# Gated linear attention and MLP in one kernel: the first four blocks loaded as two pairs with two tokens a partition, the squared activations laid out by block

## The chip, the core and the metric

The kernel runs on one core of one Trainium2 chip. The metric is the device time of one execution in microseconds, the median of several runs. The engines are named as in the profile: PE (matmul), PEld (its weight loads), DVE (vector), ACT (scalar, activation functions), POOL (GpSimd), SP (issues most DMAs). PSUM is the memory that PE writes, in banks of 512 fp32 columns.

## The reference

Four batches of eight heads, 768 tokens, 48 values a head. A recurrent state is decayed row by row with alpha and updated by k and v; its product with q goes, heads side by side, into an MLP with a squared ReLU.

```python
batch, n_heads, seq, head_dim = (4, 8, 768, 48)
n_tokens, d_model, d_ff = (3072, 384, 2048)
for t in range(S):
    state = alpha[:, :, t, :, None] * state + np.einsum('bhd,bhe->bhde', k[:, :, t], v[:, :, t])
    y[:, :, t] = np.einsum('bhd,bhde->bhe', q[:, :, t], state)
x = y.transpose(0, 2, 1, 3).reshape(B * S, H * D)
h = x @ w_in
r = np.maximum(h, 0.0)
g = s * (r * r) + b
out = g @ w_out
```

## The kernel before

The 3,072 tokens are cut into 24 **blocks** of 128 tokens, six to a batch. A token of a block lies on each partition. For every block:

- SP loads alpha, q, k, v with one DMA each into `a_in` to `v_in` (L192, five buffers each, `NIN`). One DMA moves 192 KB in 1,024 pieces of 192 bytes, a head's 48 fp32 values of one token.
- ACT takes the logarithm (L299), PE sums it over the tokens with a triangular matrix and makes the block's total decay `bl` with small matmuls (L304), both in PSUM bank `ct_ps`. ACT makes b = exp(sum), 1/b and exp(total) (L319, L322).
- DVE multiplies q by b and k by 1/b into `qk` (L332, L337). Both are transposed into `qkT`: blocks 0 to 7 (`NPE`) on PE through `ct_ps` with a copy by DVE (L345, L372), later ones by a DMA that ACT issues (L354).
- POOL casts v into `vp` (L326). PE multiplies k and v for the state update into bank `py_ps` (KV, L360); DVE adds it to the state (t1, L380), POOL applies the decay (L396).
- PE makes the scores in `a_ps` (A, L402), DVE masks them (L414), PE multiplies by v and adds the state's part, again in `py_ps` (y, L433). ACT evicts y to `xd` (L466), the MLP's input. From block 9 on (`NAY`), y of a block is issued just behind A of the next one.

The MLP runs over **groups** of one or two blocks (`GROUPS`, L18), whose `xd` has three buffers. A *unit* of mm1 (L484) is one PSUM bank of 512 columns, four feature tiles of 128 for a group of one block (matmuls of 128 columns) or two for a group of two (256 columns). ACT applies the ReLU (L498), DVE squares (L501), one instruction for each feature tile, into `gt`: sixteen tiles, one for each feature tile, each a ring of 12 blocks. mm2 (L509) takes four feature tiles at a time (a quarter) and accumulates 384 columns in one of two `o_ps` banks; DVE scales and adds the bias (L522), SP stores (L534).

Weights come through four staging buffers `wst` of 768 KB, are cast by ACT (L247, L260), and for w_out DVE also sums them over the rows for the bias (L267 to L273), which two fp32 matmuls then finish (L285).

The order is written by a small planner (`Schedule`, L43): every operation has an engine, an assumed duration, a priority and the names it reads and writes; the planner runs this list in its own time and issues the instructions in the order found. The priorities are `want(n)`, from the block's number, `UNIT` and `LEAD`, plus an offset for each kind of operation in `P`. SP's loads have their order from `LOADS` and then from the block's number; stores have a high priority and stand in SP's queue where the planner saw their data ready. Each engine executes its queue in order. Where PE would be idle early on, the planner adds filler matmuls on zeros into `o_ps[0]` (L684).

Of the kernel before, what the change touches and what calls it, by code (L numbers as in the profile page):

```python
# [15 lines left out]
VW = 144  # L16

GROUPS = [2, 1, 1, 2, 2, 2, 2, 2, 2, 2, 2, 2, 2]  # L18
UNIT = 0.756
LEAD = {1: 98.3, 2: 224.9, 4: 115.8}  # L20

NPE = 8

NAY = 9
# [5 lines left out]
TB = 1.02  # L30
TW = 2.15
FILL_GAP = 0.45

P_BM, P_CS, P_BMM = -5, -380.7, 485.1
P = dict(
    ln=-4.98, cum=7.29, eb=-25.15, ei=-13.19, vc=29.56, qb=-11.01, kb=-39.87, T=15.87,
    Tc=-9.38, KV=-36.89, t1=-9.91, sn=53.95, Ay=-1.22, A=-16.47, mk=-35.05, y=52.89,
    ye=4.82, m1=-13.73, re=-0.8, sq=-9.48, m2=-14.41, oe=20.18,
)

LOADS = ["k1", "q1", "a1", "i0", "k2", "v1", "i1", "a2", "i2", "q2", "i3", "v2", "a3", "q3", "k3", "o0", "v3", "a4", "o1", "o2", "k4", "o3", "q4", "z0", "v4"]
# [92 lines left out]
def kernel(  # L134
# [16 lines left out]
    C = 128  # L151
    NCH = S // C
# [17 lines left out]
    p_ps = py_ps[:, 0:384].rearrange("a (p e) -> a p e", p=NP)  # L170
    y_ps = py_ps[:, 0:384].rearrange("a (k t) -> a k t", k=3)
    h_ps = [ps.tile([128, 512], FP32, name=f"h_ps{i}") for i in range(2)]
    o_ps = [ps.tile([128, 512], FP32, name=f"o_ps{i}") for i in range(2)]

# [9 lines left out]

    a_in = many("a_in", NIN, [128, H, D], FP32)
# [4 lines left out]
    b_col = sb.tile([128, 1], FP32, name="b_col")  # L190

# [7 lines left out]
    for src, dst in ((alpha, a_in), (q, q_in), (k, k_in), (v, v_in)):  # L199
        load(0, src, dst)  # L200
    nc.scalar.preload_act_table_set("natural_log_exp_and_others")

    la_sb = many("la", 2, [128, H, 64], BF16, zero=nc.vector)
    U_bf = sb.tile([128, 128], BF16, name="U_bf")
    make_upper_triangular(nc, U_bf, 1.0, diag=True)
    ident_bf = sb.tile([128, 128], BF16, name="ident_bf")
    make_identity(nc, ident_bf)
    zeros = sb.tile([128, 512], BF16, name="zeros")
    nc.vector.memset(zeros, 0.0)
    ones_col_bf = sb.tile([128, 1], BF16, name="ones_col_bf")  # L210
    nc.vector.memset(ones_col_bf, 1.0)
    vp_sb = many("vp", 4, [128, NP, VW], BF16, zero=nc.gpsimd)
    mask = sb.tile([128, 128], BF16, name="mask")
    make_upper_triangular(nc, mask, 1.0, diag=True)
    b_sb = many("b_s", 2, [128, H, D], FP32)
    binv_sb = many("binv", 2, [128, H, D], FP32)
    qk_sb = many("qk", 3, [128, 2, H, 64], BF16, zero=nc.vector)
    qkT_sb = many("qkT", 3, [128, 2, NP, 128], BF16)
    am_sb = many("am", 2, [128, 2, NP, 128], BF16)
    blast_sb = many("blast", 2, [128, NP], BF16)  # L220
    t1_sb = many("t1", 2, [128, NP, 96], BF16, zero=nc.gpsimd)
    s_sb = many("s_st", 3, [128, NP, 96], BF16, zero=nc.gpsimd)
    xd_sb = many("xd", 3, [128, 3, 512], BF16)
    r_sb = many("r", 2, [128, 512], BF16)
    gt_sb = [sb.tile([128, RING * C], BF16, name=f"gt{j}") for j in range(NJ)]
# [49 lines left out]

    def load_bs():
        nc.sync.dma_start(out=b_col, in_=moe_b.to_broadcast((128, 1)))
        nc.sync.dma_start(out=s_col, in_=moe_s.to_broadcast((128, 1)))
# [6 lines left out]
    def bias_mm():  # L285
        for e in range(2):
            nc.tensor.matmul(
                out=o_ps[1][:, 0:d_model],
                lhsT=bones,
                rhs=colsum[:, d_model * e : d_model * (e + 1)],  # L290
                start=(e == 0),
                stop=(e == 1),
            )

    def bias_copy():
        nc.vector.tensor_copy(out=bias_w, in_=o_ps[1][:, 0:d_model])
# [7 lines left out]
    def st_cum(n):  # L304
        la = la_sb[n % 2]
        nc.tensor.matmul(  # L306
            out=cum_ps, lhsT=U_bf, rhs=la[:, :, 0:D], start=True, stop=True
        )
        laf = la.rearrange("a h d -> a (h d)")
        for p in range(NP):  # L310
            nc.tensor.matmul(  # L311
                out=bl_ps[:, p : p + 1],
                lhsT=laf[:, 128 * p : 128 * p + 128],
                rhs=ones_col_bf,
                start=True,
                stop=True,
            )
# [4 lines left out]
    def st_exp_i(n):  # L322
        nc.scalar.activation(out=binv_sb[n % 2], in_=cum_ps, func=AF.Exp, scale=-1.0)  # L323
        nc.scalar.activation(out=blast_sb[n % 2], in_=bl_ps, func=AF.Exp)
# [7 lines left out]
    def st_qb(n):  # L332
        nc.vector.tensor_tensor(  # L333
            out=qk_sb[n % 3][:, 0, :, 0:D], in0=q_in[n % NIN], in1=b_sb[n % 2], op=ALU.mult
        )

    def st_kb(n):  # L337
        nc.vector.tensor_tensor(  # L338
            out=qk_sb[n % 3][:, 1, :, 0:D],
# [5 lines left out]
    def st_T(n):  # L345
        f = qk_sb[n % 3].rearrange("a x h d -> a (x h d)")
# [7 lines left out]
    def st_Tdma(n):  # L354
        nc.scalar.dma_start_transpose(  # L355
            out=qkT_sb[n % 3].rearrange("a x p t -> a (x p) t"),
            in_=qk_sb[n % 3].rearrange("a x h d -> a (x h d)"),
        )

    def st_KV(n):  # L360
        kb = qk_sb[n % 3][:, 1].rearrange("a h d -> a (h d)")
        vp = vp_sb[n % 4].rearrange("a p (x d) -> a p x d", d=D)
        for p in range(NP):
            nc.tensor.matmul(  # L364
                out=p_ps[:, p, :],
# [6 lines left out]
    def st_Tcopy(n):  # L372
        nc.vector.tensor_copy(  # L373
            out=qkT_sb[n % 3].rearrange("a x p t -> a (x p t)"),
# [5 lines left out]
    def st_t1(n):  # L380
        bl = blast_sb[n % 2].unsqueeze(2).to_broadcast([128, NP, D])
        for e in range(2):
            r, c = slice(64 * e, 64 * e + 64), slice(D * e, D * e + D)
            if n % NCH == 0:
                nc.vector.tensor_tensor(
                    out=s_sb[n % 3][r, :, c], in0=p_ps[r, :, c], in1=bl[r], op=ALU.mult
                )
            else:
                nc.vector.tensor_tensor(  # L389
                    out=t1_sb[n % 2][r, :, c],  # L390
                    in0=p_ps[r, :, c],
# [10 lines left out]
    def st_A(n):  # L402
        qkT = qkT_sb[n % 3]
# [10 lines left out]
    def st_mask(n):  # L414
# [3 lines left out]
            in1=mask.unsqueeze(1).to_broadcast([128, H, 128]),  # L418
# [14 lines left out]
    def st_y(n):  # L433
        first = n % NCH == 0
        qT = qkT_sb[n % 3][:, 0]
# [6 lines left out]
        for i, (p, e, x) in enumerate(parts):  # L442
            c0 = 32 * x - 96 * p
            nc.tensor.matmul(  # L444
                out=y_ps[32 * (x % 4) : 32 * (x % 4) + 32, x // 4, :],
# [15 lines left out]

    blk_group = []
# [3 lines left out]
    def st_yevac(n):  # L466
        g, t = blk_group[n]
        nc.scalar.activation(  # L468
            out=xd_sb[g % 3][:, :, t * C : (t + 1) * C], in_=y_ps, func=AF.Copy
        )  # L470
# [30 lines left out]
    def square(w):  # L501
        g, js = units[w]
        n = GROUPS[g] * C
        c0 = first_blk[g] % RING * C
        for i, j in enumerate(js):
            r = r_sb[w % 2][:, i * n : (i + 1) * n]
            nc.vector.tensor_tensor(out=gt_sb[j][:, c0 : c0 + n], in0=r, in1=r, op=ALU.mult)  # L507

    def mm2(x):  # L509
        g, tt, jq = quads[x]  # L510
        op = o_ps[(x // 4) % 2]
        c0 = (first_blk[g] + tt) % RING * C
        for j in range(4 * jq, 4 * jq + 4):
            nc.tensor.matmul(  # L514
                out=op[:, 0:d_model],
                lhsT=gt_sb[j][:, c0 : c0 + C],
# [40 lines left out]
    SRC = {"a": (alpha, a_in), "q": (q, q_in), "k": (k, k_in), "v": (v, v_in)}  # L557
    loads = list(LOADS)
    for n in range(1, NBLK):
# [4 lines left out]

    stage = 0
    for x in range(4):
        op("SP", 1.4 if x == 0 else 0.85, -2000 + x, lambda: None, w=[("aqkv"[x], 0)], lat=2.0)
    for rank, item in enumerate(loads):
        t, i = rank - 1000, int(item[1:])
        if item[0] in "aqkv":  # L570
            if i < NIN:
# [18 lines left out]
    op("PE", 1.3, P_BMM, bias_mm, r=["bones", "colsum"], w=[("o", 1)], lat=0.16)  # L590
    op("DVE", 0.53, -300, bias_copy, r=[("o", 1)], w=["bias"])

    ys = {}

    def yevac_op(n):
        g = blk_group[n][0]
        op("ACT", 0.41, want(n) + P["ye"], st_yevac, n, r=["py"], w=[("xd", g % 3, blk_group[n][1])])
# [3 lines left out]
    def add_block(n):  # L601
        i2, i3, ii = n % 2, n % 3, n % NIN
        t = want(n)
        if n >= NIN:
# [6 lines left out]
        op("POOL", 0.5, t + P["vc"], st_vcast, n, r=[("v", ii)], w=[("vp", n % 4)], lock=True)  # L611
        op("DVE", 0.48, t + P["qb"], st_qb, n, r=[("q", ii), ("b", i2)], w=[("qb", i3)], lock=True)
        op("DVE", 0.48, t + P["kb"], st_kb, n, r=[("k", ii), ("bi", i2)], w=[("kb", i3)], lock=True)
        if n < NPE:
            op("PE", 0.45, t + P["T"], st_T, n, r=[("qb", i3), ("kb", i3)], w=["ct"], lat=0.16)
            op("DVE", 0.61, t + P["Tc"], st_Tcopy, n, r=["ct"], w=[("qkT", i3)])
        else:
            op("ACT", 1.25, t + P["T"], st_Tdma, n, r=[("qb", i3), ("kb", i3)],
               w=[("tq", i3), ("qkT", i3)], lat=0.1)
# [101 lines left out]
```

## Time and profile before

| | us |
|---|---|
| median of 7 runs (range) | 194.19 (193.9 to 194.84) |
| the profiled execution | 194.22 |
| its span, from first to last instruction | 192.3 |
| mm1 matmuls (L490) busy, x624 | 75.0 |
| mm2 matmuls (L514) busy, x384 | 72.6 |
| squares (L507, DVE) busy, x208 | 54.1 |
| ReLU (L499, ACT) busy, x96 | 56.1 |
| first mm1 matmul starts | 18.98 |

The busy time of matmuls holds overlaps, since they are pipelined: the distance between the starts of two neighbours is what one costs. The DMA section of the page shows loads of 192 KB with 3.8 to 4.4 us from issue to landing, weight loads of 768 KB with 7.6 to 7.9, and 117,536 of 124,218 packets under 512 bytes. The mean granted PE clock is 0.991.

### The profile page before, as it was taken

Reading aid. Unit: us, or ns where it says so; the run is one execution under the profiler, and the core shown is the slowest. Engines: PE = TensorE matmul, PEld = TensorE weight load, DVE = VectorE, ACT = ScalarE, POOL = GpSimd, SP = SyncE. Lnnn points to the kernel's source line nnn. Section 1 sums busy time; section 2 is a strip of 40 time slices with the busy share of each in tenths; the row PEclk is TensorE's granted clock in tenths of the full one; section 3 lists DMA queues with packets and bytes.
Section 4 is the critical chain, followed back from the end, with each engine's and each line's share of the span. In section 5 each row is a group of like instructions: output and inputs, shape, how many; then the busy total and the mean of one; then the engine's idle time right before and its main releaser. Section 6 shows DMA issues by size and latency. Waiting matters only on the chain.

```text
span 192.3 us, 5473 instructions
## 1 busy us (share of the span) xinstructions
PE 175.5 (91%) x2153; PEld 126.5 (66%) x2153; DVE 145.5 (76%) x368; ACT 109.0 (57%) x225; POOL 33.6 (17%) x60
## 2 busy tenths in 40 slices
PE   1885988979999999999999989999999999999992
PEld 1454766656677767677776667776776776777660
DVE  4742489999999999878788769778789787745421
ACT  4255779975356837278457538573674563664300
POOL 8411021123111420200122112100311321000000
PEclk9999699999999999999999999999999999999999
DMA  6999899999799999899898999997989884101112
GB/s 127 236 273 316 236 248 279 342 175 195 160 239 180 211 202 196 181 207 224 164 232 93 193 193 230 180 204 132 242 170 206 164 180 99 41 3 43 41 47 80
DMA packets 124218, 34.44 MB, mean 179 GB/s; under 512 B 117536, under 2 KB 122656, under 8 KB 124192
## 3 DMA queue, kind: packets, MB, share of 16 engines
q1 hardware_dynamic: 107296, 29.89, 69.2%
q10 hardware_dynamic: 16896, 4.20, 14.5%
q8 instruction: 17, 0.28, 0.6%
q14 instruction: 9, 0.07, 0.1%
HBM read 25.17 MB, written 4.72 MB: 155 GB/s over the span
## 4 chain that ended last, share of the span: by engine, by line
PE 61%; DVE 16%; DMA 7%; SPq 6%; ACT 3%; issue 3%; ACTq 2%; DVEq 0%
PE o_ps L514 25%; PE h_ps L490 24%; DVE gt L507 6%; DMA wst<-in_moe_w_in_dram 4%; PE py_ps L444 4%; SPq L194 4%; DMA k_in<-in_k_dram 3%; PE a_ps L406 3%; SPq L240 2%; DVE am L415 2%; DVE t L389 2%; PE py_ps L364 2%; ACTq L355 2%; PE ct_ps L306 2%; ACT r L499 1%
## 5 line engine op out<-in xcount | busy, mean ns | idle before, releaser
L490 PE MATMUL h_ps<-xd,w_in_bf 128*128 128x256 bf16 (+1 forms) x624 | 75.0, 267 | 2.1 <-ACT r L499 2.0
L499 ACT ACTIVATE r<-h_ps 128x512 bf16<-128x512 f32 x96 | 56.1, 599 | 35.8 <-PE h_ps L490 19.3
L514 PE MATMUL o_ps<-w_out_bf,gt 128*128 128x384 bf16 x384 | 72.6, 326 | 1.2 <-ACT w_out_bf L261 1.2
L507 DVE TENSOR_TENSOR gt<-r 128x256 bf16<-128x256 bf16 (+1 forms) x208 | 54.1, 310 | 14.8 <-ACT r L499 14.3
L490 PEld LDWEIGHTS <-w_in_bf 128*128 128x128 bf16 x624 | 55.6, 98 | 13.1 <-issue 2.8
L514 PEld LDWEIGHTS <-gt 128*128 128x128 bf16 x384 | 35.9, 98 | 20.2 <-issue 1.5
L415 DVE TENSOR_TENSOR am<-a_ps,mask 128x1024 bf16<-128x1024 f32 x24 | 29.3, 1221 | 2.6 <-PE a_ps L406 2.3
L327 POOL CAST vp<-v_in 128x384 bf16<-128x384 f32 x24 | 14.1, 586 | 72.3 <-DMA v_in<-in_v_dram 57.6
L400 POOL TENSOR_TENSOR s_st<-t,blast 128x384 bf16<-128x384 bf16 x16 | 14.2, 887 | 53.0 <-DVE t L389 24.8
L300 ACT ACTIVATE la<-a_in 128x384 bf16<-128x384 f32 x24 | 12.5, 520 | 13.7 <-DMA a_in<-in_alpha_dram 8.3
L525 DVE SCALAR_TENSOR_TENSOR o_sb<-o_ps,s_col,bias_w 128x384 f32<-128x384 f32 x24 | 14.8, 615 | 6.3 <-PE o_ps L514 6.0
L338 DVE TENSOR_TENSOR qk<-k_in,binv 128x384 bf16<-128x384 f32 x24 | 13.4, 557 | 6.5 <-ACT binv L323 4.4
L333 DVE TENSOR_TENSOR qk<-q_in,b_s 128x384 bf16<-128x384 f32 x24 | 13.3, 553 | 5.8 <-ACT b_s L320 4.6
L468 ACT ACTIVATE xd<-py_ps 128x384 bf16<-128x384 f32 x24 | 11.8, 492 | 10.0 <-PE py_ps L444 7.6
L320 ACT ACTIVATE b_s<-ct_ps 128x384 f32<-128x384 f32 x24 | 11.8, 491 | 8.5 <-PE ct_ps L311 7.1
L389 DVE TENSOR_TENSOR t<-py_ps,s_st 64x192 bf16<-64x192 f32 x32 | 11.3, 352 | 4.4 <-PE py_ps L364 3.1
L306 PE MATMUL ct_ps<-la,U_bf 128*128 128x384 bf16 x24 | 8.1, 335 | 6.4 <-POOL mask masks.py:65 4.1
L323 ACT ACTIVATE binv<-ct_ps 128x384 f32<-128x384 f32 x24 | 11.8, 491 | 0.0
L311 PEld LDWEIGHTS <-la 128*128 128x128 bf16 x96 | 6.0, 98 | 7.4 <-issue 5.5
L406 PE MATMUL a_ps<-qkT 64*128 64x128 bf16 x192 | 9.7, 222 | 1.2 <-DVE qkT L373 1.2
L406 PEld LDWEIGHTS <-qkT 64*128 64x128 bf16 x192 | 5.5, 95 | 7.7 <-issue 5.1
L444 PE MATMUL py_ps<-am,vp 128*32 128x128 bf16 x384 | 9.6, 219 | 0.7 <-DVE am L415 0.7
(42 smaller groups left out, 106.6 us busy)
## 6 DMA issues: line engine op xcount, KB each, us to landing
a_in<-in_alpha_dram SPq DMA_DIRECT2D x24, 192.0 KB, 4.3
q_in<-in_q_dram SPq DMA_DIRECT2D x24, 192.0 KB, 4.2
k_in<-in_k_dram SPq DMA_DIRECT2D x24, 192.0 KB, 3.8
v_in<-in_v_dram SPq DMA_DIRECT2D x24, 192.0 KB, 4.4
out_dram<-o_sb SPq DMA_DIRECT2D x24, 192.0 KB, 2.1
wst<-in_moe_w_in_dram SPq DMA_DIRECT2D x4, 768.0 KB, 7.9
wst<-in_moe_w_out_dram SPq DMA_DIRECT2D x4, 768.0 KB, 7.6
qkT<-qk ACTq DMA_TRANSPOSE x16, 4.5
```

The costliest lines, as they stand in the source:

```text
L327: nc.gpsimd.tensor_copy(out=vp_sb[n % 4].rearrange("a p (x d) -> a p x d", d=D)[:, :, 0:3:2, :], in_=v_in[n % NIN].rearrange("a (p e) d -> ...
L338: nc.vector.tensor_tensor(out=qk_sb[n % 3][:, 1, :, 0:D], in0=k_in[n % NIN], in1=binv_sb[n % 2], op=ALU.mult,)
L389: nc.vector.tensor_tensor(out=t1_sb[n % 2][r, :, c], in0=p_ps[r, :, c], in1=s_sb[(n - 1) % 3][r, :, c], op=ALU.add,)
L400: nc.gpsimd.tensor_tensor(out=s_sb[n % 3], in0=t1_sb[n % 2], in1=bl, op=ALU.mult)
L406: nc.tensor.matmul(out=a_ps[:, e, p, :], lhsT=qkT[64 * e : 64 * e + 64, 1, p, :], rhs=qkT[64 * e : 64 * e + 64, 0, p, :], start=True, stop ...
L415: nc.vector.tensor_tensor(out=am_sb[n % 2].rearrange("a e p t -> a (e p) t"), in0=a_ps.rearrange("a e p t -> a (e p) t"), in1=mask.unsquee ...
L444: nc.tensor.matmul(out=y_ps[32 * (x % 4) : 32 * (x % 4) + 32, x // 4, :], lhsT=(st[:, p, c0 : c0 + 32] if e is None else vp[:, p, c0 + 48 ...
L490: nc.tensor.matmul(out=hp[:, i * n : (i + 1) * n], lhsT=w_in_bf[:, kk, 128 * j : 128 * (j + 1)], rhs=xd_sb[g % 3][:, kk, 0:n], start=(kk = ...
L499: nc.scalar.activation(out=r_sb[w % 2], in_=h_ps[w % 2], func=AF.Relu)
L507: nc.vector.tensor_tensor(out=gt_sb[j][:, c0 : c0 + n], in0=r, in1=r, op=ALU.mult)
L514: nc.tensor.matmul(out=op[:, 0:d_model], lhsT=gt_sb[j][:, c0 : c0 + C], rhs=w_out_bf[:, j, :], start=(j == 0), stop=(j == NJ - 1),)
L525: nc.vector.scalar_tensor_tensor(out=ots, in0=o_ps[(x // 4) % 2][:, 0:d_model], scalar=s_col, in1=bias_w, op0=ALU.mult, op1=ALU.add,)
```

## The change

The first four blocks are handled as two **pairs** of blocks (256 tokens). Partition s of a pair holds tokens 2s and 2s + 1, so one DMA moves 384 KB in pieces of 384 bytes (`load_pair`). Block c of the pair is then on partitions 64c to 64c + 63, with even tokens in slot j = 0 and odd ones in j = 1. The pairs' buffers lie inside `gt`, in ring slots 9 to 11 and 6 to 8, which are written by squares only later.

What follows for a pair: one ln over both, cumulative sums with two new triangular matrices in `a_ps`, three exps, one product each for q and for k (`pair_mul`), 16 transposes through `ct_ps` and a second bank, two copies by DVE that put the columns in block order with even tokens first. v is cast in four pieces of 64 partitions; half of it has to change partitions for y, which two DMAs on POOL's queue do (`pair_vmove`). KV of a block of a pair is eight matmuls over 64 rows instead of four over 128. The mask is `mask2`, for even tokens first; ACT's eviction of y puts the tokens back in order.

Further: `gt` becomes one tile laid out block, feature tile, token, so that one instruction squares a whole unit of 512 columns. The groups are 2, six of 1, four of 2, 1, three of 2, 1. KV goes to `ct_ps` from block 8 on, y of blocks 0 and 1 to `o_ps[1]`. `qk` and `qkT` have four buffers instead of three. The last block of a batch makes no state update and no total. PE transposes up to block 6, the joint A and y starts at block 8. The planner's numbers and the order of loads are new: both pairs, the weights, then block 4; and the planner takes a store's data for ready 2.5 us later (`LATE`), so that stores stand later in SP's queue. The bias sums are folded first, and one matmul finishes them.

```diff
-GROUPS = [2, 1, 1, 2, 2, 2, 2, 2, 2, 2, 2, 2, 2]
-UNIT = 0.756
-LEAD = {1: 98.3, 2: 224.9, 4: 115.8}
-NPE = 8
-NAY = 9
+GROUPS = [2, 1, 1, 1, 1, 1, 1, 2, 2, 2, 2, 1, 2, 2, 2, 1]
+UNIT = 0.87
+LEAD = {1: 132.3, 2: 36.1, 4: 356.0}
+NPE = 7
+NAY = 8
+LATE = 2.5
+NY = 2
+NKV = 8
+NR2 = 2
...
-LOADS = ["k1", "q1", "a1", "i0", "k2", "v1", "i1", "a2", "i2", "q2", "i3", "v2", "a3", "q3", "k3", "o0", "v3", "a4", "o1", "o2", "k4", "o3", "q4", "z0", "v4"]
+LOADS = ["K0", "A0", "K1", "Q0", "A1", "i0", "v4", "Q1", "V0", "i1", "V1", "i2", "i3", "o0", "o1", "o2", "o3", "k4", "q4", "z0", "a4"]
...
+    def y_of(n):
+        return (o_ps[1] if n < NY else py_ps)[:, 0:384].rearrange("a (k t) -> a k t", k=3)
+    def p_of(n):
+        return (ct_ps if n >= NKV else py_ps)[:, 0:384].rearrange("a (p e) -> a p e", p=NP)
+    gt_sb = sb.tile([128, RING, NJ, C], BF16, name="gt")
-    gt_sb = [sb.tile([128, RING * C], BF16, name=f"gt{j}") for j in range(NJ)]
+    def pair_in(m):
+        r = 9 - 3 * (m % 2)
+        raw = gt_sb[:, r : r + 3].rearrange("a r j t -> a (r j t)").bitcast(FP32)
+        return raw.rearrange("a (x h j d) -> a x h j d", x=4, h=H, j=2)
+    def load_pair(m, x, src):
+        b, c = 2 * m // NCH, 2 * m % NCH
+        nc.sync.dma_start(
+            out=pair_in(m)[:, x].rearrange("a h j d -> a h (j d)"),
+            in_=src[b, :, c * C : (c + 2) * C, :].rearrange("h (s j) d -> s h (j d)", j=2),
+        )
...
+    def pair_mul(m, x):
+        s = 2 * m % 4
+        nc.vector.tensor_tensor(
+            out=qk_all[:, s : s + 2, x, :, 0:D],
+            in0=pair_in(m)[:, 1 + x].rearrange("a h j d -> a j h d"),
+            in1=(binv_all if x else b_all),
+            op=ALU.mult,
+        )
...
+    def pair_vmove(m, c):
+        a, b = HC * c, HC * (1 - c)
+        nc.gpsimd.dma_start(out=vp_sb[(2 * m + c) % 4][b : b + HC], in_=vc_sb[m % 2][a : a + HC])
...
     def square(w):
         g, js = units[w]
-        n = GROUPS[g] * C
-        c0 = first_blk[g] % RING * C
-        for i, j in enumerate(js):
-            r = r_sb[w % 2][:, i * n : (i + 1) * n]
-            nc.vector.tensor_tensor(out=gt_sb[j][:, c0 : c0 + n], in0=r, in1=r, op=ALU.mult)
+        m, s0 = GROUPS[g], first_blk[g] % RING
+        r = r_sb[w % 2].rearrange("a (i s t) -> a i s t", i=len(js), s=m)
+        nc.vector.tensor_tensor(
+            out=gt_sb[:, s0 : s0 + m, js[0] : js[0] + len(js)].rearrange("a s j t -> a j s t"),
+            in0=r,
+            in1=r,
+            op=ALU.mult,
+        )
...
             if jq == 3:
                 op("DVE", 0.54, t + P["oe"], oevac, x, r=[("o", ob), "bias", "s"],
-                   w=[("os", (x // 4) % 3)])
+                   w=[("os", (x // 4) % 3)], lat=LATE if x < len(quads) - 40 else 0.08)
```

## Prediction

> **What bounds the kernel now.** I read the engines' shares first, then the span in stretches, then the chain that ended last.
>
> ```profile
> PE 175.5 (91%) x2153; PEld 126.5 (66%) x2153; DVE 145.5 (76%) x368; ACT 109.0 (57%) x225; POOL 33.6 (17%) x60
> ```
> ```profile
> 0.00:10.00 10.00, 5.02 (x52) 3.22 (x52) 5.84 (x13) 3.27 (x6) 6.04 (x21) 1.00 0.85 188
> 10.00:20.00 10.00, 6.86 (x100) 5.16 (x92) 3.56 (x6) 6.05 (x11) 1.33 (x2) 0.94 1.00 295
> 20.00:30.00 10.00, 9.08 (x107) 6.90 (x105) 7.57 (x18) 7.78 (x16) 1.34 (x2) 0.89 0.94 237
> 30.00:40.00 10.00, 8.40 (x132) 6.38 (x130) 9.90 (x29) 9.42 (x16) 1.36 (x2) 1.00 0.99 290
> 40.00:50.00 10.00, 8.88 (x119) 6.37 (x117) 9.89 (x29) 5.38 (x10) 3.15 (x3) 1.00 0.91 184
> ...
> 115.00:140.00 25.00, 25.00 (x322) 18.23 (x320) 21.00 (x52) 15.49 (x37) 3.96 (x6) 1.00 1.02 197
> ```
>
> Columns: stretch, length, busy us of PE, weight loads, DVE, ACT and POOL, PE clock, DMA share, GB/s. PE is full from 50 us on; before that it is not, although filler matmuls on zeros count as busy. So I price the useful matmuls by their distance start to start in the timeline: 162.5 ns for 384 columns, 109 ns for 256, 56 ns for 128 (mm1 in blocks of one). mm2: 384 x 0.1625 = 62.4 us. mm1: 528 x 0.109 + 96 x 0.056 = 62.9 us. Attention and bias, priced alike: 29.7 us. Together **155.0 us of a 192.3 us span**. Counting the same matmuls up to 50 us gives 25.0 us of work there, so 25.0 us are lost by then; from 50 us to the last matmul at 188.6 us another 8.6; the tail (eviction, last store) is 3.7. The change can win in the first 25 and in part of the 8.6.
>
> The chain names what ends the waits of the start:
>
> ```profile
> 12.50 8.22 DMA wst<-in_moe_w_in_dram
> 20.74 1.48 ACT w_in_bf L248
> ...
> 37.89 0.62 DVE gt L507 x4
> 38.52 0.87 DVE colpart L269
> ```
>
> Until 22 us it runs through transfers and weight casts, from 33 to 46 us through DVE, which is 99% busy there. Later there are single holes:
>
> ```profile
> SPq L537 <- DVE o_sb L525: 68.7, 23, 9.6
> ```
> ```profile
> 105.37 0.36 SPq L537 DMA_DIRECT2D out_dram<-o_sb  x1
> 105.78 0.43 SPq L194 DMA_DIRECT2D q_in<-in_q_dram  x1
> 106.25 0.69 SPq L194 DMA_DIRECT2D k_in<-in_k_dram  x1
> ...
> 111.55 0.56 DVE L338 TENSOR_TENSOR qk<-k_in,binv 128x384 bf16<-128x384 f32 x1 [2.07 <-DMA k_in<-in_k_dram]
> ```
>
> SP stands at an output store that waits for DVE, the loads stand behind it, and q and k come late. By the same pricing 100 to 115 us loses 2.4 us and 70 to 80 us 1.1, where quiet stretches lose 0.4 in 10 us.
>
> **Matmul work.** Eight groups of one block instead of two: +288 matmuls of 128 columns (+16.1 us), -144 of 256 (-15.7). Transposes on PE fall from 64 to 56 (-0.45); one more block goes through ACT's DMA transpose. Pair cumulative sums: +4 matmuls of 384 columns, -16 tiny ones, +0.25. One fp32 bias matmul instead of two (four passes of 323 ns in the trace, two now): -0.65. Sum about -0.5: **work 154.5 us**.
>
> **Loads of the first four blocks.** A pair load has the same 1,024 pieces as a block load, each 384 instead of 192 bytes. The first seven block loads land from 3.42 to 9.00 us, 0.93 us each; a 768 KB weight load takes about 2.65 us. Bounds for a pair load: 0.93 (a piece costs the same) and 1.86 (twice). A line through 192 bytes (14.5 ns a piece and engine) and 2,048 bytes (110 ns) gives 24 ns, 1.56 us. The Trainium skill, DMA: Bandwidth & Descriptors, Specifications, says that pieces under 512 bytes miss the line rate; 384 still do, so by it the pair load gains little: 1.86, i.e. 8 x 0.3 = 2.4 us later than at 1.56. I take 1.5, nearest the line. Then, with v4 and four weight loads between: A0 lands at 4.0, V0 8.5, A1 11.5, first w_in part 14.2, Q1 16.6, second part 19.2, V1 20.7, third and fourth 23.4 and 26.0, w_out 28.6 to **36.6** (before: 39.85), a4 39.4. The w_in parts come up to 2.7 us later than before (20.7 and 23.6), w_out 3.3 earlier.
>
> **Chain of the first pair**, from rows: ln on 768 columns 0.85 (0.52 for 384), to 4.85; cumulative sum at the cold rate (the first fillers take 0.24 us, later ones 0.12) 1.4, to 6.3; exp 0.85 twice, to 8.1; two products of 0.95 (0.56 for half), to 9.1; 16 transposes 1.2; two PSUM copies of 0.69 (strided now: 0.5 to 1.0 each), to 11.3; scores, two masks of 1.22 with state sums of 0.73 between, to 15.0. The second pair's sums share a_ps with the masks, so they start at 15.0; its exps on ACT end at 18.0, and the eviction of block 1 stands behind them: first mm1 at 18.6, where it was 18.98. Nothing is won there, but blocks 2 and 3 are then half done; before only block 2 was begun.
>
> **V of the pairs.** Four casts of about 0.5 us, then two copies over POOL's DMA queue for the half that sits on the other partitions. No such DMA is in the trace; the nearest rows are stores, 2.1 us to landing, and ACT's transposes, 4.5. I take 3: issued at 10.5, landed at 13.5, when y(0) is due (13.7). Against it stands the Trainium skill, SBUF — State Buffer, A bandwidth-pool intuition that's wrong: such a DMA of 0.62 us took 3.1 beside a DVE instruction that held the shared port. The row that bears on it:
>
> ```profile
> 41.95 1.88 POOL L327 CAST vp<-v_in 128x384 bf16<-128x384 f32 x1 [7.05 <-DMA v_in<-in_v_dram]
> ```
>
> It is 0.50 elsewhere, so POOL is held up by DVE here too. By the row's 1.4 us on top, y(0) slips to 15.1, the pair sums behind it on PE by 0.5; by the page's 2.5, 16.2 and 1.6 us. Either is mostly covered by ACT's wait for the third w_in part (23.4), so I put 0; uncovered it costs up to 1.6.
>
> **DVE.** Squares: 0.155 us for 128 columns (0.62 for four), 0.24 for 256 (0.48 for two); extended, 0.37 for 512, bounds 0.31 and 0.48. 208 of 54.1 us become 96 of 36. Steadily that lies beside PE. From 17 to 46 us DVE has, row by row as built, about 22 us of work: no longer the bound. What is late next is ACT: from 18.6 us seven casts (10.4), eleven ReLUs (6.6) and three evictions (1.5), plus waits for weights: last cast done at 38.1, two ReLUs after it 39.3. By then PE has done attention of four blocks (7.2), 11 units (7.2) and four quarters of mm2 (2.6): 17.0 of 39.3 us, **22.3 lost**; before it was about 22.7 there. From there 5 units and 12 quarters (11.2 us) are ready, until 50.5, and block 4, its alpha landed at 39.4, is done by 47.5. So PE stays full: 22.8 lost at 50 us instead of 25.0, **-2.2**.
>
> **Steady part.** Stores are planned 2.5 us later (LATE), so fewer loads stand behind one; KV moves to ct from block 8 on, away from y's bank. SP's and POOL's queues otherwise keep their work. The holes at 70-80 and 100-115 are 2.5 us above the quiet rate; a new fixed order makes holes of its own, so I take half: **-1.2** (bounds -2.5 and +6). Tail unchanged: the last 36 matmuls (5.9 us) cover the last ReLU and square.
>
> Sum against the profiled execution: 194.22 (span 192.3 + 1.9 around) - 0.5 - 2.2 - 1.2 = **190.3**; the median, 194.19, is the same time.
>
> **Rivals.**
> - **Pieces cost the same** (0.93 a pair load, chance 0.18): all loads up to V1 come up to 4.6 us earlier, weights and alpha of block 4 too, and PE is full at 36 instead of 39: 187.2. For it: three quarters of the early time is DMA-bound. Against: the line above.
> - **The start only shifts its wait** (0.12): pair load 1.86 and copies at 4.5 us give back the 2.2, new holes the 1.2: 193.7, by matmul work alone.
> - **Slower: groups of one shorten the reach** (0.20). Six more boundaries where mm1 can run ahead of attention by one block instead of two (xd has three buffers, whatever the group's size). Where a load is late as at 106 us, all of PE stands. A row of such a stand is 0.89 us (mm1 waiting for a ReLU at 114.6). From 0.65 us at each of six boundaries on it eats the whole 3.9; at the row's 0.89, six take 5.3: 195.6. For it: DMA share is 1.0 until 140 us, so a late load isn't caught up. Against: singles are smaller bites and the loads now lead by 3 us.
>
> **Numbers.** Forecast 0.50, own range 188.5 to 192.3. About 0.3% (0.6 us) is what a measurement of this kernel can tell from no change. The second rival splits into 0.05 faster and 0.06 within, the slower one keeps 0.20: faster 0.73, same 0.06, slower 0.21. The range, 186.6 to 195.0, leaves out the far half of the slower case and a tail below.
>
> **What would show it.** Right: a4's ln near 40 us, the last w_out cast ending near 38, PE without fillers or holes from 40 us on, squares near 0.37 us, SP without waits over 4 us in front of loads. Wrong: first mm1 after 20 us, y(0) waiting for POOL's copy, DVE still 99% busy at 30 to 45 us, or holes of 1 us at block boundaries between 50 and 110 us.

## The result and the profile after

The changed kernel takes **189.94 us** (median of 12 runs, 188.2 to 191.01) where the kernel before, run beside it on the same chip, takes 194.22 (31 runs, 192.82 to 196.18): a ratio of **0.9772**, 95% interval 0.9743 to 0.9802. Ratios, here and below, leave out executions more than 1.5% above the fastest of the same kernel. The profiled execution took 189.79 us, with a span of 188.1.

The engines' shares first, with the group of the squares (line, engine, tile, count, busy us, mean ns, idle time before it and what ended it) from the page of the changed kernel:

```profile
PE 173.5 (92%) x2259; PEld 127.0 (68%) x2259; DVE 134.5 (72%) x252; ACT 107.7 (57%) x213; POOL 41.7 (22%) x71
...
PE 57%; DMA 7%; DVE 2%; issue 1%; ACT 0%; ACTq 0%
...
L677 DVE TENSOR_TENSOR gt<-r 128x512 bf16<-128x512 bf16 x96 | 43.4, 466 | 18.2 <-ACT r L671 17.4
```

96 squares of 466 ns in the mean take 43.4 us where 208 took 54.1, and DVE falls by 11.0 us. Of the chain that ended last, DVE holds 2%.

The span in stretches (stretch, length, busy us of PE, PEld, DVE, ACT, POOL, granted PE clock, DMA share, GB/s):

```profile
0.00:10.00 10.00, 4.34 (x26) 2.67 (x27) 3.11 (x9) 3.71 (x5) 8.36 (x25) 1.00 0.91 250
10.00:20.00 10.00, 7.78 (x110) 5.17 (x109) 5.50 (x9) 4.20 (x6) 4.48 (x9) 0.70 1.08 339
20.00:30.00 10.00, 9.61 (x131) 7.58 (x128) 8.68 (x14) 9.01 (x12) 4.34 (x6) 0.96 0.99 334
30.00:40.00 10.00, 8.57 (x122) 6.45 (x120) 9.59 (x17) 9.14 (x14) 1.53 (x1) 1.00 0.78 186
40.00:50.00 10.00, 10.00 (x148) 7.45 (x147) 8.86 (x19) 6.33 (x15) 2.15 (x3) 1.00 0.99 205
...
115.00:140.00 25.00, 24.95 (x332) 17.85 (x330) 18.36 (x35) 14.28 (x32) 3.71 (x6) 1.00 0.98 179
```

PE is full from 40 us on; before it was full from 50. Up to 30 us the transfers run at 250 to 339 GB/s instead of 188 to 295. At 30 to 40 us they fall to 186; the last weights land at 33.87. One number is worse: the PE clock of 10 to 20 us is 0.70 instead of 0.94 (0.50 from 14.0 to 20.8 us). Priced as in the prediction, useful matmuls make 154.5 us; 21.8 us are lost by 50 us (before 25.0), and 8.1 from there to the last matmul (before 8.6).

Single rows of the start, from the timeline (start, duration, engine, line, operation, tiles; in brackets the idle time before it and its releaser):

```profile
7.90 2.28 POOL L608 CAST vc<-gt 64x384 bf16<-64x384 f32 x2 [0.33 <-DMA gt<-in_v_dram]
...
15.79 0.35 PEld L515 LDWEIGHTS <-vp 128*32 128x32 bf16 x16 [0.40 <-DMA vp<-vc]
...
21.30 0.82 PE L662 MATMUL h_ps<-xd,w_in_bf 128*128 128x256 bf16 x6
...
35.28 1.57 ACT L322 ACTIVATE w_out_bf<-wst 128x1536 bf16<-128x1536 f32 x1
...
38.49 0.52 ACT L368 ACTIVATE la<-a_in 128x384 bf16<-128x384 f32 x1 [0.67 <-DMA a_in<-in_alpha_dram]
```

First mm1 comes at 21.30 us, later than before (18.98). The last cast of w_out ends at 36.85 (before 41.35), the logarithm of block 4's alpha at 39.01. SP's waits, in us in total, times, longest:

```profile
SPq L712 <- DVE o_sb L700: 34.0, 12, 6.8
SPq L712 <- DVE gt L677: 25.2, 8, 7.2
SPq L316 <- ACT w_in_bf L309: 9.1, 3, 4.2
SPq L712 <- DVE s_st L460: 6.4, 3, 2.9
```

L712 is the output store. In the three rows that name DVE it still waits 65.6 us, against 68.7 before; the longest wait is 7.2 instead of 9.6.

### The profile page after: what moved, and what is told of

Read it like the earlier page. It is cut to its first block, busy times and chain, and to the rows that moved or that the text cites. A ratio compares the mean times of both kernels' runs of the same rounds, so it can differ in the third digit from the quotient of the medians.

```text
span 188.1 us, 5557 instructions
## 1 busy us (share of the span) xinstructions
PE 173.5 (92%) x2259; PEld 127.0 (68%) x2259; DVE 134.5 (72%) x252; ACT 107.7 (57%) x213; POOL 41.7 (22%) x71
## 4 chain that ended last, share of the span: by engine, by line
PE 57%; DMA 7%; DVE 2%; issue 1%; ACT 0%; ACTq 0%
PE o_ps L689 25%; PE h_ps L662 22%; DMA qkT<-qk 7%; PE py_ps L515 4%; PE a_ps L477 3%; PE ct_ps L374 1%; PE ct_ps L435 1%; DVE o_sb L700 1%; DVE qk L404 1%; PE ct_ps L381 0%; DVE qk L409 0%; ACTq L426 0%; ACT b_s L390 0%; DVE gt L677 0%; ACT blast L395 0%
## 5 line engine op out<-in xcount | busy, mean ns | idle before, releaser
L671 ACT ACTIVATE r<-h_ps 128x512 bf16<-128x512 f32 x96 | 56.1, 606 | 28.2 <-PE h_ps L662 21.4
L662 PEld LDWEIGHTS <-w_in_bf 128*128 128x128 bf16 x768 | 58.8, 98 | 9.3 <-issue 1.2
L677 DVE TENSOR_TENSOR gt<-r 128x512 bf16<-128x512 bf16 x96 | 43.4, 466 | 18.2 <-ACT r L671 17.4
L471 POOL TENSOR_TENSOR s_st<-s_st,blast 128x384 bf16<-128x384 bf16 x16 | 14.3, 897 | 59.8 <-DVE s_st L460 35.9
L368 ACT ACTIVATE la<-a_in 128x384 bf16<-128x384 f32 x20 | 10.5, 523 | 10.3 <-DMA a_in<-in_alpha_dram 4.5
L404 DVE TENSOR_TENSOR qk<-q_in,b_s 128x384 bf16<-128x384 f32 x20 | 11.6, 582 | 1.8 <-ACT b_s L390 1.8
L409 DVE TENSOR_TENSOR qk<-k_in,binv 128x384 bf16<-128x384 f32 x20 | 11.3, 567 | 1.0 <-ACT binv L393 1.0
L393 ACT ACTIVATE binv<-ct_ps 128x384 f32<-128x384 f32 x20 | 9.8, 489 | 3.6 <-PE ct_ps L381 2.9
L460 DVE TENSOR_TENSOR s_st<-ct_ps,s_st 64x192 bf16<-64x192 f32 x22 | 7.8, 352 | 2.5 <-PE ct_ps L435 2.2
L577 DVE TENSOR_TENSOR qk<-gt,binv 128x768 bf16<-128x768 f32 x2 | 1.9, 958 | 8.2 <-ACT binv L570 8.2
L515 PEld LDWEIGHTS <-vp 128*32 128x32 bf16 x384 | 6.7, 100 | 1.1 <-DMA vp<-vc 0.8
```

The source lines that it names most:

```text
L404: nc.vector.tensor_tensor(out=qk_sb[n % 4][:, 0, :, 0:D], in0=q_in[n % NIN], in1=b_sb[n % 2], op=ALU.mult)
L409: nc.vector.tensor_tensor(out=qk_sb[n % 4][:, 1, :, 0:D], in0=k_in[n % NIN], in1=binv_sb[n % 2], op=ALU.mult,)
L471: nc.gpsimd.tensor_tensor(out=s_sb[n % 3], in0=t1_sb[n % 2], in1=bl, op=ALU.mult)
L515: nc.tensor.matmul(out=y_of(n)[32 * (x % 4) : 32 * (x % 4) + 32, x // 4, :], lhsT=(st[:, p, c0 : c0 + 32] if e is None else vp[:, p, c0 + ...
L662: nc.tensor.matmul(out=hp[:, i * n : (i + 1) * n], lhsT=w_in_bf[:, kk, 128 * j : 128 * (j + 1)], rhs=xd_sb[g % 3][:, kk, 0:n], start=(kk = ...
L671: nc.scalar.activation(out=r_sb[w % 2], in_=h_ps[w % 2], func=AF.Relu)
```

## The experiments

My theory after the result: the gain comes from the start, where longer pieces bring the weights in earlier. Rivals: the relief of DVE is the gain (fewer squares); the late stores are; groups of one cost something that the rest pays for. Each run is timed against the kernel before on its own chip, whose median moved between 194.22 and 195.8 us, so ratios are compared. One per cent is 1.94 us of the kernel before, and the differences below are differences of ratios. "Same order" means that every engine has its instructions in the changed kernel's (or the kernel before's) order; "planned anew" means that the planner made another order, which is a change of its own.

**1. Short pieces again.** Each pair load as two loads of 192-byte pieces, same order.

```diff
-        nc.sync.dma_start(
-            out=pair_in(m)[:, x].rearrange("a h j d -> a h (j d)"),
-            in_=src[b, :, c * C : (c + 2) * C, :].rearrange("h (s j) d -> s h (j d)", j=2),
-        )
+        for j in range(2):
+            nc.sync.dma_start(
+                out=pair_in(m)[:, x, :, j],
+                in_=src[b, :, c * C : (c + 2) * C, :].rearrange("h (s j) d -> s h j d", j=2)[:, :, j],
+            )
```

> The changed kernel (189.9 us), but each pair load is two DMAs of 192-byte pieces, one per token of the two; order of everything else as in the changed kernel. Theory (the early loads gain by their longer pieces): two short loads take 2 x 0.93 us instead of one of 1.20, so the eight pair loads end about 5 us later and the last w_out part lands near 38.5 us instead of 33.9; DVE and ACT being ready by then, the time rises by 2 to 3.5 us, to 192 to 193.5, still under the 194.2 of the kernel before. Rival (relief of DVE is the gain, loads have slack): under 1 us more, below 191. Rival (loads are all of it): 194 or more.

Ratio 1.0205 (1.0138 to 1.0272): 4.3% or 8.4 us above the changed kernel, and slower than the kernel before. Theory and first rival gave too little; by its number the rival "loads are all of it" is nearest. Two rows of its timeline show what I had left out:

```profile
19.54 0.62 PE L516 MATMUL o_ps<-am,vp 128*32 128x128 bf16 x16 [2.26 <-DMA vp<-vc]
...
24.98 0.82 PE L663 MATMUL h_ps<-xd,w_in_bf 128*128 128x256 bf16 x6
```

The last w_out part lands at 40.88 us instead of 33.87, 7 us later and not 5; and the copies of V now land at 19.49 and 20.01 us, since the short loads are still in the way. y(0) waits 2.26 us for them and first mm1 slips from 21.30 to 24.98.

**2. No pairs.** The first four blocks as single blocks, in the load order of the kernel before, the setup of what only pairs need left out; planned anew.

```diff
-NR2 = 2
+NR2 = 0
-LOADS = ["K0", "A0", "K1", "Q0", ...
+LOADS = ["k1", "q1", "a1", "i0", ...
-        load_pair(0, x, src)
+        load(0, src, (a_in, q_in, k_in, v_in)[x])
```

> The changed kernel without pairs: the first four blocks loaded and treated as single blocks with 192-byte pieces, loads in the order of the kernel before, planned anew; one square a unit, groups, late stores and banks as in the changed kernel. Theory (the start is 3 of the 4.3 us won): w_out lands near 40 us again, 24.5 to 25.5 us lost by 50 us, ratio 0.990 to 1.000. Rival (pairs only pay for their own extra work): ratio 0.975 to 0.985.

Ratio 0.9973 (0.994 to 1.0007): 2.0%, 3.9 us, of the gain are gone, within the theory's range. By 50 us 28.2 us are lost, more than the 24.5 to 25.5 expected. PE's rows tell why:

```profile
33.01 0.81 PE L668 MATMUL o_ps<-w_out_bf,gt 128*128 128x384 bf16 x4 [1.24 <-ACT w_out_bf L301]
...
37.60 0.81 PE L668 MATMUL o_ps<-w_out_bf,gt 128*128 128x384 bf16 x4 [1.04 <-ACT w_out_bf L301]
...
39.35 0.82 PE L668 MATMUL o_ps<-w_out_bf,gt 128*128 128x384 bf16 x4 [0.94 <-ACT w_out_bf L301]
```

Three quarters of mm2 wait for the casts of w_out, whose last part lands at 40.53 us. In the changed kernel the same three waits are 0.22, 0.54 and 0.20 us. But the kernel before, with the same order of loads and its last part at 39.85, loses only 25.0 us by 50 us. So 3.2 of the 28.2 come from what else is different here, as the plan and the groups, and not from the loads, and the 3.9 us are not the pairs' alone; the order of loads, which changes with them, was not tried apart. Set beside the first run, pairs with short pieces are 2.3% slower than no pairs. With the same reservation, the pair's own detours cost some 4.5 us and the longer pieces give back 8.4.

**3. One square for each feature tile again,** in the changed kernel, same order.

```diff
-        nc.vector.tensor_tensor(
-            out=gt_sb[:, s0 : s0 + m, js[0] : js[0] + len(js)].rearrange("a s j t -> a j s t"),
-            in0=r, in1=r, op=ALU.mult)
+        for i, j in enumerate(js):
+            nc.vector.tensor_tensor(
+                out=gt_sb[:, s0 : s0 + m, j], in0=r[:, i], in1=r[:, i], op=ALU.mult
+            )
```

> The changed kernel, but one square for each feature tile again (16 x 4 or 2 instructions a group as before), same planned order. Theory: DVE is not the bound after 20 us any more because w_out comes earlier, and steadily squares lie beside PE; DVE gets about 10 to 20 us busier and the time rises by 0.5 to 1.5 us. Rival (relief of DVE is the gain of the change): rises by 3 us or more, to 193 or above, with DVE 99% busy from 30 to 45 us again. Rival (no part in it): within 0.3 us.

Ratio 0.9903 (0.9871 to 0.9934): 1.3%, 2.5 us slower than the changed kernel, outside the theory's 0.5 to 1.5 and short of the rival's 3. The stretches show the rival's sign, DVE full again:

```profile
30.00:40.00 10.00, 8.64 (x125) 6.60 (x124) 9.88 (x26) 9.14 (x12) 1.53 (x1) 1.00 0.83 200
40.00:50.00 10.00, 9.07 (x128) 6.44 (x124) 9.88 (x39) 6.14 (x14) 1.83 (x3) 1.00 1.00 205
```

Of PE's time 23.1 us are lost by 50 us instead of 21.8; more is lost later. For the part before 50 us this fits DVE as the next bound once the weights are early.

**4. One square for a unit alone,** in the kernel before, with `gt` by block; same order. (The edit is that of `square`, `mm2` and the tile in the change's diff.)

> The kernel before (194.2 us), with gt laid out by block and one square for a unit, nothing else; planned order as before. Theory: the squares go to about 0.47 us, DVE has less to do at 30 to 46 us, but the last w_out part lands at 39.9 us as before and its cast and sums follow it, so PE is full only some 1 us earlier: 193.2 to 194.2. Rival (relief of DVE is the gain): 191.5 or less.

Ratio 0.9933 (0.9898 to 0.9968), 1.3 us: a gain, slightly above the theory's and far from the rival's. In its profile the time lost by 50 us (25.5) is not less than before: its chain of waits lies in the transfer of the last w_out part from 31.9 to 41.1 us, so the weights are still the bound there.

**5. Stores at once,** planned anew.

```diff
-LATE = 2.5
+LATE = 0.08
```

> The changed kernel with stores planned at once (0.08 us) instead of 2.5 us later; the planner makes a new order, which moves PE work from about 70 us on too. Theory (stores in front of loads make the later holes): SP's waits at stores grow again to near the 69 us of the kernel before and holes of 1 to 2 us come back where a load stands behind one: 190.5 to 192, none of it before 50 us. Rival (stores have no part, or the new order decides): within 0.5 us of the changed kernel, or any change without a wait for a load in it.

Ratio 1.0036 (0.9989 to 1.0082): 2.6%, 5.1 us above the changed kernel, no gain left at all. That is far more than either side gave. Up to 50 us the profile is that of the changed kernel (21.8 us lost); the holes come after it. SP's queue, then DVE's and PE's rows of the largest one, from the timeline:

```profile
72.29 0.53 SPq L218 DMA_DIRECT2D a_in<-in_alpha_dram  x1
78.43 0.36 SPq L712 DMA_DIRECT2D out_dram<-o_sb  x1
78.83 0.43 SPq L218 DMA_DIRECT2D q_in<-in_q_dram  x1
79.31 0.70 SPq L218 DMA_DIRECT2D k_in<-in_k_dram  x1
```
```profile
86.38 0.56 DVE L409 TENSOR_TENSOR qk<-k_in,binv 128x384 bf16<-128x384 f32 x1 [3.10 <-DMA k_in<-in_k_dram]
```
```profile
88.97 1.47 PE L662 MATMUL h_ps<-xd,w_in_bf 128*128 128x256 bf16 x12 [1.47 <-ACT r L671]
```

Read from the top: after 72.82 us SP stands at a store until DVE has evicted at 78.4. q and k are queued behind it; k, issued at 79.31, lands at 86.35, its product starts then, the transpose on ACT's queue and the ReLU behind that follow, and PE loses 3.1 us between 80 and 90. The stand is not all of it: k takes 7.0 us to land, where the median of such loads is 4.2. What slowed it was not taken apart.

**6. Stores early in the changed kernel's order.** Run 5 moved everything; here only SP's queue changes: each store stands right behind its eviction's place.

```diff
-        for i in sorted(range(len(self.ops)), key=lambda i: (begin[i], i)):
+        at = list(begin)
+        for i, o in enumerate(self.ops):
+            if o[3].__name__ == "ostore":
+                at[i] = max(self.end[d] for d in o[5])
+        for i in sorted(range(len(self.ops)), key=lambda i: (at[i], i)):
```

> The changed kernel with every instruction of PE, DVE, ACT and POOL in the order of the changed kernel; only in SP's queue each output store stands right behind the place where the planner puts its eviction, ahead of the one to three loads that the 2.5 us had let pass. The run with 0.08 us and a new plan was 2.6% slower than the changed kernel by ratio (1.004 against 0.977). Theory A (a store that waits holds back the loads behind it): most of this comes back without a new plan, ratio to the kernel before 0.992 to 1.004, with holes where k or q lands late. Theory B (the new plan of the other engines did it): ratio 0.975 to 0.983.

Ratio 0.9922 (0.9889 to 0.9955), just inside theory A: 1.5%, 2.9 us, are the stores' places in the queue. The rest of run 5, 1.1%, is left for the new plan; that is a difference between runs on two chips.

**7. Stores late in the kernel before,** same order.

```diff
+        at = list(begin)
+        for i, o in enumerate(self.ops):
+            if o[3].__name__ == "ostore" and o[4][0] < 56:
+                at[i] = begin[i] + 2.5
```

> The kernel before, all engines in their order, only each store but the last ten moved behind the loads that the planner puts into the next 2.5 us of its time. Theory A (late stores are a gain by themselves): the holes at 100 to 115 us (2.4 us lost) and 70 to 80 us go, 1 to 2 us less, ratio 0.990 to 0.995. Theory B (late stores only mend what the change itself brings in): ratio 0.998 or more.

Ratio 0.9976 (0.994 to 1.0012), between the two and not told from no change. The holes did shrink in its profile (100 to 120 us lose 1.5 instead of 2.7, 70 to 80 us 0.7 instead of 1.1), but 0.5 us more are lost by 50 us. So late stores are worth 2.9 us in the changed kernel; in the one before it is 0.5, with an interval from a loss of 0.2 to a gain of 1.2.

**8. The groups of the kernel before,** in the changed kernel; planned anew.

```diff
-GROUPS = [2, 1, 1, 1, 1, 1, 1, 2, 2, 2, 2, 1, 2, 2, 2, 1]
+GROUPS = [2, 1, 1, 2, 2, 2, 2, 2, 2, 2, 2, 2, 2]
```

> The changed kernel with the groups of the kernel before (2, 1, 1, then ten of 2), planned anew. Theory (groups of one are near neutral in the work, +0.4 us for their 288 more matmuls, and let mm1 start after one block): within 1.5 us of the changed kernel, ratio 0.970 to 0.985. Rival (groups of one cost at their boundaries, the slower case of the forecast): 2 us or more faster than the changed kernel, ratio below 0.967. Rival (groups of one are a part of the gain): ratio above 0.988.

Ratio 0.9893 (0.9834 to 0.9951): on the side of the last rival, 1.2% slower than the changed kernel, but the interval is wide and the order is a new one. There is no sign that groups of one cost 2 us; that they bring 2.4 is not shown either.

**9. More fillers.** All other work in the changed kernel's order, 57 filler matmuls in the profile instead of 29, until 17 us of the planner's time into a bank that nobody waits for.

```diff
+        dst = h_ps[1] if at < 17.0 else o_ps[0]
-        for _ in range(int((idle - FILL_GAP) / (0.22 if at < 9.0 else 0.12))):
+        for _ in range(int((idle - 0.05) / (0.22 if at < 9.0 else 0.11))):
```

> The changed kernel with more filler matmuls in the first 20 us (54 instead of 29) and into a bank that nobody waits for; all other work in its order. Theory (the granted clock of 0.50 from 13.9 to 20.6 us comes from PE's gaps there and lengthens the chain): the clock of 10 to 20 us rises from 0.70 to above 0.9, pair 1's sums take about 0.9 us instead of 1.6, first mm1 starts near 20.4 us instead of 21.3 and the time falls by 0.4 to 1.0 us, ratio 0.972 to 0.975. Rival (the start is set by transfers and casts): first mm1 earlier or not, time within 0.3 us, ratio 0.976 to 0.979.

Ratio 0.9775 (0.9738 to 0.9813): the rival, no change. The stretches of the changed kernel, then of this one:

```profile
12.50:15.00 2.50, 1.64 (x25) 1.13 (x24) 1.93 (x4) 1.48 (x1) 0.00 (x0) 0.80 1.11 305
15.00:17.50 2.50, 2.07 (x27) 1.08 (x27) 1.84 (x4) 0.60 (x1) 1.27 (x2) 0.50 1.01 310
17.50:20.00 2.50, 2.50 (x42) 1.72 (x41) 0.43 (x1) 1.28 (x3) 0.88 (x2) 0.50 1.09 392
```
```profile
12.50:15.00 2.50, 2.39 (x29) 1.49 (x27) 2.38 (x6) 1.40 (x1) 0.00 (x0) 1.00 1.13 310
15.00:17.50 2.50, 2.20 (x49) 1.41 (x52) 1.22 (x1) 0.74 (x2) 1.27 (x2) 1.00 1.11 328
17.50:20.00 2.50, 2.50 (x41) 2.17 (x37) 1.79 (x2) 2.50 (x5) 1.34 (x2) 1.00 1.08 372
```

The clock is 1.00 in all three, and first mm1 starts at 19.57 us instead of 21.30, even earlier than expected. Not all of that is the clock, since the run also changes the fillers' bank. The changed kernel first, then this one:

```profile
12.19 0.27 PE L925 MATMUL o_ps<-zeros,ident_bf 128*128 128x256 bf16 x1 [0.93 <-DVE qkT L603]
...
12.39 0.21 PE L624 MATMUL py_ps<-vp,qk 64*128 64x96 bf16 x1
```
```profile
11.69 0.21 PE L624 MATMUL py_ps<-vp,qk 64*128 64x96 bf16 x1
```

`o_ps[0]` holds half of the pair's transposes. In the changed kernel a filler into it waits for DVE's copy, and KV, next in PE's queue, starts 0.7 us later than here, before the clock falls.

What does the earlier start bring? The last w_out part lands at 33.31 instead of 33.87, and of 1.7 us only 0.6 are left at 50 us in the profile and none that the times can tell. Nor do the twelve runs of the changed kernel go by their mean clock: 189.11 us at 0.969, 191.01 and 188.2 at 0.991.

**10. The bias sums on PE.** DVE's seven fp32 additions, their folding and the bias product go (7.2 us from 28 to 40 us); PE sums w_out's bf16 rows with a matrix of ones, into the bank that the fp32 matmul used.

```diff
+        if 4 <= x < 8:
+            for j in range(4 * jq, 4 * jq + 4):
+                nc.tensor.matmul(
+                    out=o_ps[0][:, 0:d_model], lhsT=ones_bf, rhs=w_out_bf[:, j, :],
+                    start=(j == 0), stop=(j == NJ - 1))
```

> The changed kernel with the bias sums taken from DVE (7.2 us of fp32 additions between 28 and 40 us, and the bias product) and made by 16 bf16 matmuls with ones behind the first four quarters of mm2; other work in its order. +2.6 us of PE work, -0.65 us of the fp32 matmul. Theory (from 28 to 40 us ACT's casts and ReLUs are the bound after the change, DVE only just behind): PE pays its 2 us partly in its holes, time 0 to +1.5 us, ratio 0.977 to 0.985. Rival (DVE is still the bound there, 96% busy): 1 us or more faster, ratio below 0.973.

Ratio 0.9827 (0.979 to 0.9865): 0.5%, 1.1 us slower, as the theory said. Its stretch from 30 to 40 us:

```profile
30.00:40.00 10.00, 9.44 (x122) 6.95 (x119) 3.92 (x8) 8.93 (x12) 0.83 (x1) 1.00 0.83 193
```

DVE is busy for 3.92 us instead of 9.59, ACT for 8.93 as before, and the last w_out cast ends no earlier (37.60 instead of 36.85). So DVE was hardly the bound there any more. The run also adds some 1.9 us to PE and is 1.1 us slower, so a gain of up to 0.8 us could hide in it.

**11. Both, and six staging buffers.**

```diff
-NST = 4
+NST = 6
```

> Both of these and six staging buffers for weights instead of four. Theory: SP no longer stands at the w_out loads for casts of w_in (9.1 us of waiting), the last w_out part lands near 31.5 us instead of 33.9 and the loads of block 4 before 37; the casts on ACT follow by 1 to 2 us, ratio 0.966 to 0.976. Rival (transfers are not the bound after 22 us): as the sum of the two others.

Ratio 0.9821 (0.9771 to 0.9871): the rival, the sum of runs 9 and 10. SP no longer waits for casts, yet the w_out parts land at 27.0 to 34.3 us, not before those of the changed kernel (26.0 to 33.9), whose DMA share is 0.99 from 20 to 30 us already: SP's 9.1 us of waiting cost nothing, because the transfers ahead were still running. The buffers also bring a wait of their own. All four w_out loads are now issued ahead of the copies of the second pair's V; these are issued at 23.08 us and land at 29.58 and 30.17, 6.5 us after their issue instead of 5.3, and hold up block 2's y. So the run does not show what the buffers would be worth without that.

**12. As 11, with two of the four w_out casts on POOL.**

```diff
     def cast_w_out(i, st):
+        if i in (0, 2):
+            nc.gpsimd.tensor_copy(
+                out=w_out_bf[:, 4 * i : 4 * i + 4], in_=wst[st].rearrange("a (j m) -> a j m", j=4)
+            )
+            return
```

> As the one before, with two of the four w_out casts on POOL, which is idle there, in the same place of the order. Theory (ACT is the bound from 20 to 38 us): 3 us less on ACT, PE full some 2 us earlier, ratio 0.957 to 0.970. Rival (a cast on POOL beside DVE takes 4 us or more and holds up the state update behind it on POOL): ratio not below the one before.

Ratio **0.9687** (0.9642 to 0.9732), 189.53 us beside 195.25: theory, 1.3% better than run 11 and 0.9% better than the changed kernel, whose interval it does not touch. It is the fastest version that I have. A cast on POOL, and what the V copies cost here, from the timeline:

```profile
27.21 1.46 POOL L320 CAST w_out_bf<-wst 128x1536 bf16<-128x1536 f32 x1 [1.80 <-DMA wst<-in_moe_w_out_dram]
...
29.68 0.35 PEld L503 LDWEIGHTS <-vp 128*32 128x32 bf16 x16 [3.26 <-DMA vp<-vc]
```

The cast takes 1.46 us, as on ACT (1.48). The weights of y(2) still wait 3.26 us for the copies. The profiled execution took 192.61 us, the longest of the six, so it does not show where the time was won. That the two moved casts win it follows from the difference between runs 11 and 12; that they do so by relieving ACT is the likely reading and not shown. POOL's casts in the changed kernel without the other edits were not tried; by runs 9 to 11 the others bring nothing or cost.

## Why the prediction was right, and where it was not

The time and its sign were right: 190.3 predicted, 189.94 measured. The sum had three terms, and their errors went against each other: start -3.2 instead of -2.2, later part -0.5 instead of -1.2. That 190.3 came so close is in part luck. Of its own signs of being right two failed, squares near 0.37 us (0.466) and no wait of SP over 4 us in front of loads (7.2); two signs of being wrong came, the late first mm1 and y(0) waiting for POOL's copy.

- **Work:** 154.5 us predicted, 154.5 measured.
- **A pair load:** 1.5 us taken, bounds 0.93 and 1.86. The first four land at 4.25, 5.40, 6.61 and 7.84 us: 1.20 each. The Trainium skill (DMA: Bandwidth & Descriptors, Specifications) puts the least size for the full rate at 512 bytes; I had weighed this as hardly any gain at 384 (1.86 us). The trace has 1.20 us for 384 KB against 0.93 for 192 KB, so the pair loads move 328 GB/s where block loads move 211 and weight loads, at the forecast's 2.65 us, 297. The weights behind them land 1.2 to 2.7 us earlier than I had it (last w_out part 33.87 instead of 36.6). This term is mis-sized, and it is the likely source of the larger gain at the start: by 39.3 us PE had done thirteen units of mm1 and not eleven, 18.6 us of work instead of 17.0.
- **First mm1 at 18.6 us:** wrong, 21.30. Two steps of the pair's chain failed. I took PE's cold rate once, for the first sums, and the warm rate after it; but the clock was 0.50 from 14.0 to 20.8 us. And I gave no cost to the fillers, which the chain waits for. The rows of run 9 split its 1.7 us: 0.7 is the filler that waits for DVE's copy, 0.65 is the sums of pair 1 (from their start to the first exp 1.74 us instead of 1.09), and 0.4 is mm1 standing behind eleven fillers, these too at half rate. The other 1.0 stays in run 9. There the copies of the first pair end at 12.1 us instead of 11.3, and the first mask stands behind a state sum of 0.74 us that I had counted only between the masks. I had also called a first mm1 after 20 us a sign against the forecast. It was none: run 9 brings it back to 19.57 and wins nothing.
- **V's copies at no cost:** right in the outcome, wrong in the cover. They landed 4.5 us after their issue, at my upper bound, after two casts that took 2.28 us beside DVE's products instead of 1.0 (the next two, with DVE idle for the first half, 1.06). Of the additions that I had weighed, 1.4 and 2.5 us, the trace has 1.5 over my 3; it does not show whether DVE's port is the cause. y(0) waited 0.4 us; but pair 1's sums were held until 16.9 us by the masks, not ACT by the third w_in part, and that is what hid it. Where loads are in front of them, the copies cost 2.26 us (run 1) and 3.26 (run 12).
- **PE full at 39 us, ACT late next:** right (39.85). That ACT and not DVE is the bound from 20 to 38 us is what runs 10 and 12 point to.
- **Squares:** 0.37 us taken, 0.31 to 0.48 as bounds, 0.466 measured. The trace tells why. Two rows of squares and one of POOL from the timeline:

```profile
29.44 0.42 DVE L677 TENSOR_TENSOR gt<-r 128x512 bf16<-128x512 bf16 x1
31.16 1.53 POOL L471 TENSOR_TENSOR s_st<-s_st,blast 128x384 bf16<-128x384 bf16 x1 [4.57 <-DVE s_st L460]
31.93 1.05 DVE L677 TENSOR_TENSOR gt<-r 128x512 bf16<-128x512 bf16 x1
```

Of the changed kernel's 96 squares, the 75 with no POOL instruction beside them take 0.41 to 0.43 us each. The 21 that overlap one take 0.42 to 1.05, 0.63 in the mean, and all twelve above 0.43 us are among these. The kernel before gave a hint: 32 squares at 0.155 and 176 at 0.24 make 47 us, not the 54.1 that stand beside these prices in the prediction. "Steadily that lies beside PE", so nothing was counted after 50 us: too simple. Run 3 costs 2.5 us, and between its profiled execution (194.85 us, its longest) and that of the changed kernel only 1.3 of 5.1 us lie before 50 us.
- **Late stores, half of the 2.5 us of holes:** the size was near (-0.5 instead of -1.2), the mechanism was not. I read them as a cure for the holes of the kernel before. There they are worth 0.5 us, not told from nothing (run 7); in the changed kernel's order, taking them away costs 2.9 (run 6).
- **Rivals:** pieces at equal price, no (1.20 us, not 0.93). The start only shifts its wait, no (21.8 us lost by 50 us instead of 25.0). Groups of one on the slower side, no: with the groups before the kernel is not faster (run 8). The chances given for these do not quite add up: 0.12 was split into 0.05 and 0.06, and 0.20 became 0.21.

The parts do not add up. Taken out one by one, short pieces, single squares and early stores cost 8.4, 2.5 and 2.9 us, 13.8 together, in a change that brings 4.4. Put in alone, squares and late stores bring 1.3 and 0.5. This would follow if each removes a wait that only becomes the last one when the others are gone; for the stores runs 6 and 7 say so, for the rest it is my reading. The kernel before with nothing but a new plan was not tried.

## What to carry to other kernels

A longer piece can pay below a stated limit for the full rate, as it did here at 384 bytes: read from the trace what two sizes cost, and draw the line. When several waits end close together, removing one shows little and restoring one costs much, so price a part against the state it will stand in, not against the kernel before. In a queue in order, a store that waits for its data holds up each load behind it: one stand of 5.6 us ahead of a slow load became 3.1 us lost on PE, and moving stores one to three loads later in the queue was worth 2.9 us here. A filler is not free either: one that writes into a bank which DVE still reads held up PE for 0.9 us.

## What the runs showed of the hardware

**The clock falls after short gaps, and costs a second time.** The steps of the granted clock lie on a grid of 3.41 us: 13.99 and 20.82 in the changed kernel, 116.63 and 120.05 in run 6. Against the program this grid lies elsewhere in each execution. In run 6's profile (its longest execution, 195.4 us) PE had one hole of 2.04 us, up to 115.34:

```profile
112.50:115.00 2.50, 0.81 (x36) 0.62 (x35) 0.71 (x2) 0.30 (x1) 0.43 (x1) 1.00 1.31 193
115.00:117.50 2.50, 2.16 (x18) 1.69 (x18) 2.11 (x4) 2.17 (x5) 0.00 (x0) 0.83 0.86 142
117.50:120.00 2.50, 2.50 (x10) 1.16 (x8) 0.79 (x3) 0.60 (x1) 1.42 (x2) 0.50 0.00 0
```

The clock falls when PE is busy again, and eight matmuls of mm2 take 2.56 us instead of 1.3. The Trainium skill (TensorE: Matmul & The Clock Gate, The HAM clock gate) has the half rate after a window of about 3.4 us without work, which runs freely. The grid agrees with such a window; "without work" does not. In the window before this fall PE was busy for 40% by the profile, and before the other falls of these profiles for 20 to 57%. Windows of 48 to 60% went either way: the one from 86.3 to 89.7 us in run 5, 48% busy, left the clock at 1.00. So the busy share alone does not tell, and where the grid lies decides with it whether a hole costs a second time.

**The clock column says 1.00 where there is no record yet.** In the changed kernel the first record is at 10.58 us, but the fillers of 256 columns before it are 213 ns apart, later ones 109. In run 1 PE stays at that half rate until 24.88 us (transposes 107 ns apart instead of 56), where the column has 1.00. So read the early rate from the matmuls.

**A copy from SBUF to SBUF on POOL's queue** took 4.1 and 4.5 us from issue to landing for the first pair of the changed kernel, 5.3 for the second, and 6.5 with more weight loads ahead (run 11), where I had taken 3.
